# Two small loads at the start of an attention and GEGLU kernel: the last tokens of k and v moved to the hardware queue, and a norm column made by a matmul instead of by element transfers

## The chip, the cores and the metric

One core of a Trainium2 chip. The metric is the device time of one execution in microseconds (us), given as the median of several runs. The kernel before takes 358.03 us (three runs, 357.89 to 358.11). The profile is taken of one of these runs; its span, from the first to the last instruction, is about 1.7 us shorter than the time of the same run.

## The reference

```python
def _attn_ref(q, k, v, g_norm):            # q, k, v: (8, 8, 576, 64) fp32; g_norm: (64,)
    kv = np.einsum('bhsd,bhse->bhde', k, v)
    out = np.einsum('bhsd,bhde->bhse', q, kv)
    rms = np.sqrt(np.mean(out * out, axis=-1, keepdims=True) + 1e-06)
    return (out / rms * g_norm).astype(np.float32)

# x = attention's result, as 4608 tokens x 512 channels
def _moe_ref(x, w_gate, w_val, w_out, w_res):   # (512,1536), (512,1536), (1536,512), (512,512)
    g = x @ w_gate
    gelu = 0.5 * g * (1.0 + erf(g / sqrt(2)))
    ffn_out = gelu * (x @ w_val) @ w_out
    res_gate = 1.0 / (1.0 + np.exp(-(x @ w_res)))
    return (x + res_gate * ffn_out).astype(np.float32)
```

Each batch has 576 tokens: four tiles of 128, and 64 last tokens that the kernel treats apart.

## The kernel before

The long part of the kernel is a chain of fp16 matmuls that keeps the tensor engine (PE) full. Only the start matters here: until batch 0 has passed through the attention, PE has nothing to chew. The loads of batch 0 go out on three queues. SP issues q, k and v in halves of four heads, in fp32, on a hardware queue. GpSimd issues the last tokens of k and v on the software queue, which casts to fp16 on the way. ACT issues g_norm twice: as a row, and as a column of 128 partitions with one 4-byte element in each.

```python
    def load_last_kv(b):
        for tile_, t in zip(last_kv[b % 2], (k, v)):
            nc.gpsimd.dma_start(out=tile_[0:R], in_=t[b, :, M0:S, :].rearrange("h s d -> s h d"))
    ...
    def load_first(which, t, half):
        hs = slice(half * HH, (half + 1) * HH)
        nc.sync.dma_start(out=raw[0, which][:, hs, :], in_=rows4(t, 0, hs.start, hs.stop))

    for half in range(2):
        for which, t in (("q", q), ("k", k), ("v", v)):
            load_first(which, t, half)
    load_last_kv(0)
    grow = consts.tile([1, D], FP32, name="grow")
    nc.scalar.dma_start(out=grow, in_=g_norm.unsqueeze(0))
    gcol = consts.tile([P, 1], FP32, name="gcol")
    for e in range(2):
        nc.scalar.dma_start(out=gcol[e * D : (e + 1) * D, :], in_=g_norm.unsqueeze(1))
```

The order of the first work follows. `keep_warm` issues matmuls of zeros ("fillers") that are meant to keep PE's clock up. `hold` makes GpSimd wait for the first k/v product before it issues the weights, so that these don't compete with q, k and v.

```python
    keep_warm(7)
    ...
    f_cast("q", 0, HH, nc.scalar.copy)
    f_qT(0)
    f_cast("k", 0, HH, nc.vector.tensor_copy)
    f_qT_out(0, nc.scalar.copy)
    f_qT_out(1, nc.scalar.copy)
    nc.vector.tensor_copy(out=g16, in_=gps)
    f_cast("v", 0, HH, nc.vector.tensor_copy)
    keep_warm(7)
    f_kv(0)                      # per head pair: 4 matmuls of v and k, 1 of their last tokens
    f_kv_out(0)
    ...
    hold = consts.tile([1, 1], FP16, name="hold")
    nc.gpsimd.tensor_copy(out=hold, in_=s0["kv2"][0:1, 0, 0:1])
    load_wg(0)
    load_wv(0)
    f_cast("k", HH, H, nc.gpsimd.tensor_copy)
    for i in range(1, len(WCS)):
        load_wg(i)
        load_wv(i)
```

Of the kernel before, what the change touches and what calls it, by code (L numbers as in the profile page):

```python
# [8 lines left out]
FP32 = mybir.dt.float32  # L9
# [9 lines left out]
def kernel(  # L19
# [15 lines left out]
    nc = tc.nc  # L35
    P = nc.NUM_PARTITIONS
    B, H, S, D = q.shape
# [5 lines left out]
    M0 = NJ * P  # L43
    R = S - M0
    RP = R // NJ
    HH = H // 2
    WCS = (256, 256, 512, 512)

    consts = ctx.enter_context(tc.tile_pool(name="consts", bufs=1))
# [10 lines left out]
    pattn = ctx.enter_context(tc.tile_pool(name="pattn", bufs=4, space=bass.MemoryType.PSUM))  # L60
# [11 lines left out]
    def rows4(t, b, lo, hi):  # L72
        return t[b, lo:hi, 0:M0, :].rearrange("h (p j) d -> p h (j d)", j=NJ)
# [10 lines left out]
    last_kv = [[consts.tile([P, H, D], FP16, name=f"{n}l{i}") for n in "kv"] for i in range(2)]  # L84
# [4 lines that stand above are left out]
# [33 lines left out]
    def load_wg(i):  # L122
        load_columns(wg_c, moe_w_gate, i)

    def load_wv(i):
        load_columns(wv_c, moe_w_val, i)
# [295 lines left out]
    for which in "kv":  # L422
        t = hidp.tile([P, NF, NJ * P], FP16, tag="hid", name=which + "f")
        t = t.rearrange("p a b -> p (a b)").bitcast(FP32)
        raw[0, which] = t[:, 0 : H * NJ * D].rearrange("p (h x) -> p h x", h=H)

    def load_first(which, t, half):
        hs = slice(half * HH, (half + 1) * HH)
        nc.sync.dma_start(out=raw[0, which][:, hs, :], in_=rows4(t, 0, hs.start, hs.stop))

    for half in range(2):
        for which, t in (("q", q), ("k", k), ("v", v)):
            load_first(which, t, half)
    load_last_kv(0)
    grow = consts.tile([1, D], FP32, name="grow")
    nc.scalar.dma_start(out=grow, in_=g_norm.unsqueeze(0))
    gcol = consts.tile([P, 1], FP32, name="gcol")
    for e in range(2):
        nc.scalar.dma_start(out=gcol[e * D : (e + 1) * D, :], in_=g_norm.unsqueeze(1))
    ident32 = consts.tile([P, P], FP32, name="ident32")  # L440
    make_identity(nc, ident32)

# [9 lines left out]
    nc.vector.memset(eps_col, RMS_EPS)  # L452
    ones16 = consts.tile([1, P], FP16, name="ones16")
    nc.vector.memset(ones16, 1.0)
    ident = consts.tile([P, P], FP16, name="ident")
    nc.vector.tensor_copy(out=ident, in_=ident32)

    qtr = [consts.tile([P, NP, P], FP16, name=f"qtr{i}") for i in range(2)]
    grow16 = consts.tile([1, H, D], FP16, name="grow16")
    nc.vector.tensor_copy(out=grow16, in_=grow[:, None, :].to_broadcast([1, H, D]))  # L460
    for t in last_kv[1] + qtr:
# [5 lines left out]
    def keep_warm(n):  # L467
        for _ in range(n):
            nc.tensor.matmul(idle, lhsT=zeros[:, 0:P], rhs=zeros, start=True, stop=True)
# [10 lines left out]
    def f_cast(which, lo, hi, copy):  # L480
        hs = slice(lo, hi)
        dst, src = b16_t[0, which], raw[0, which]
        if which == "v":
            copy(out=dst[:, hs, :], in_=src[:, hs, :])  # L484
        else:
            copy(
                out=dst.rearrange("p j h d -> p h j d")[:, hs, :, :],
                in_=src.rearrange("p h (j d) -> p h j d", j=NJ)[:, hs, :, :],
            )

    def f_qT(half):
        q16 = b16_t[0, "q"].rearrange("p j h d -> p j (h d)")
        for e2 in range(2):
            pr = 2 * half + e2
            first["qT", pr] = ps = pattn.tile([P, NJ, P], FP16, tag="at", name="qtp")
            for j in range(NJ):
                nc.tensor.transpose(ps[:, j, :], q16[:, j, pr * P : (pr + 1) * P], ident)

    def f_qT_out(pr, copy):
        copy(out=s0["qT"][:, :, pr, :], in_=first["qT", pr])  # L500
# [81 lines left out]

    keep_warm(7)

    g16 = consts.tile([P, C], FP16, name="g16")
    gps = pattn.tile([P, C], FP32, tag="at", name="gbp")
    nc.tensor.matmul(gps, lhsT=ones16, rhs=grow16.rearrange("p h d -> p (h d)"), start=True, stop=True)
# [3 lines that stand above are left out]
    f_qT_out(0, nc.scalar.copy)  # L591
    f_qT_out(1, nc.scalar.copy)
    nc.vector.tensor_copy(out=g16, in_=gps)
    f_cast("v", 0, HH, nc.vector.tensor_copy)
    keep_warm(7)
    f_kv(0)
# [8 lines left out]
    load_wg(0)  # L605
    load_wv(0)
    f_cast("k", HH, H, nc.gpsimd.tensor_copy)
    for i in range(1, len(WCS)):
        load_wg(i)
        load_wv(i)  # L610
# [208 lines left out]
```

## Time and profile before

| quantity, kernel before | value |
|---|---|
| median time | 358.03 us |
| span of the profiled run | 356.6 us |
| first half of v landed | 10.60 us |
| first k/v product starts | 11.37 us |
| first block of the value weights landed | 19.12 us |
| PE starts the third column block of the gate product | 25.89 us |

Two views matter most. That of busy time by stretches gives for every microsecond the busy time of PE, weight load, DVE, ACT and GpSimd, then the granted PE clock (1.00 is full speed), the DMA share (the mean over the 16 engines; it can pass 1.00) and the GB/s moved. The chain of waits gives start, length and what of the work that set the end. The prediction below shows the lines of both for the kernel before.

### The profile page before, as it was taken

What the parts mean: (1) busy time and instruction counts of PE and PEld (TensorE: products, weight loads), DVE (VectorE), ACT (ScalarE), POOL (GpSimd) and SP (SyncE); (2) the same over time, 40 slices, a digit from 0 to 9 for tenths busy, and PEclk for the clock granted to TensorE, in tenths of its full rate; (3) what the DMA queues carried; (4) which work ended last, traced back from release to release, by engine and by line L of the source; (5) the groups of instructions that cost most, each with busy time, mean ns of one, the idle gap of its engine ahead of it and who ended that gap; (6) DMA issues with size and microseconds to landing.
All of it is one profiled execution on the core that took longest, in us unless ns stands there. A gap on an engine that the chain in (4) does not pass through costs nothing.

```text
span 356.6 us, 5012 instructions
## 1 busy us (share of the span) xinstructions
PE 344.9 (97%) x1903; PEld 169.4 (48%) x1903; DVE 214.4 (60%) x425; ACT 125.7 (35%) x215; POOL 47.3 (13%) x72
## 2 busy tenths in 40 slices
PE   7869999999999999999999999999999999999995
PEld 2454465454455445544454445444544444444443
DVE  4555438877847865685569755855587544343433
ACT  3463374343236312531264224422542233223320
POOL 2563150050041003200050014000000000000000
PEclk9999999999999999999999999999999999999998
DMA  7999999289489055914896279518000500020013
GB/s 189 242 181 202 193 204 158 89 148 140 119 159 174 2 132 124 186 9 107 146 131 71 68 182 153 47 46 178 29 2 29 132 31 0 29 88 3 1 31 88
DMA packets 77835, 37.82 MB, mean 106 GB/s; under 512 B 42354, under 2 KB 73330, under 8 KB 77810
## 3 DMA queue, kind: packets, MB, share of 16 engines
q0 software_dynamic: 40848, 17.83, 39.9%
q1 hardware_dynamic: 36640, 19.53, 21.8%
q8 instruction: 15, 0.25, 0.3%
q10 hardware_dynamic: 322, 0.13, 0.2%
q14 instruction: 10, 0.08, 0.1%
HBM read 38.80 MB, written 9.44 MB: 135 GB/s over the span
## 4 chain that ended last, share of the span: by engine, by line
PE 91%; DMA 4%; DVE 1%; ACT 1%; issue 0%; SPq 0%; POOL 0%; DVEq 0%
PE gps L315 26%; PE vps L315 26%; PE fps L348 25%; PE rps L335 9%; DMA vf<-in_v_dram 2%; PE kvp L165 2%; PE op L194 2%; DMA wv<-in_moe_w_val_dram 2%; PE fps L377 1%; PE orp L212 1%; PE kvp L172 0%; ACT xT L581 0%; DVE hid L304 0%; ACT L664 0%; ACT xT L265 0%
## 5 line engine op out<-in xcount | busy, mean ns | idle before, releaser
L315 PE MATMUL gps<-xT,wg 128*128 128x512 f16 (+2 forms) x448 | 112.3, 371 | 2.3 <-ACT xT L581 1.2
L315 PE MATMUL vps<-xT,wv 128*128 128x512 f16 (+2 forms) x448 | 112.3, 371 | 0.8 <-DMA wv<-in_moe_w_val_dram 0.8
L304 DVE TENSOR_TENSOR hid<-ge,vps 128x512 f16<-128x512 f16 x108 | 73.5, 685 | 65.7 <-PE vps L315 57.7
L303 ACT ACTIVATE ge<-gps 128x512 f16<-128x512 f32 x108 | 64.5, 598 | 114.2 <-PE gps L315 105.2
L348 PE MATMUL fps<-wo,hid 128*128 128x512 f16 x420 | 96.8, 379 | 0.0
L315 PEld LDWEIGHTS <-wv 128*128 128x128 f16 x448 | 43.4, 98 | 51.2 <-DMA wv<-in_moe_w_val_dram 1.1
L348 PEld LDWEIGHTS <-hid 128*128 128x128 f16 x420 | 40.8, 98 | 47.9
L315 PEld LDWEIGHTS <-wg 128*128 128x128 f16 x448 | 42.1, 98 | 44.0 <-issue 2.7
L354 DVE SCALAR_TENSOR_TENSOR pf<-th,fps 128x512 f32<-128x512 f32 x35 | 23.8, 687 | 47.9 <-PE fps L348 47.9
L344 ACT ACTIVATE th<-rps 128x512 f32<-128x512 f32 x36 | 21.5, 598 | 79.5 <-PE rps L335 79.5
L335 PE MATMUL rps<-wr,xT 128*128 128x512 f16 x144 | 36.5, 379 | 0.0
L188 DVE TENSOR_REDUCE ss<-sq 128x8 f32<-128x512 f32 x32 | 21.5, 684 | 6.2 <-ACT sq L187 4.3
L359 DVE SCALAR_TENSOR_TENSOR osb<-pf,t 128x512 f32<-128x512 f32 x35 | 24.2, 691 | 1.1
L335 PEld LDWEIGHTS <-xT 128*128 128x128 f16 x144 | 14.1, 98 | 17.0
L187 ACT ACTIVATE sq<-op 128x512 f32<-128x512 f32 x28 | 16.8, 598 | 9.8 <-PE op L194 8.8
L705 POOL COPY hold<-qT 1x1 f16<-1x1 f16 x5 | 0.9, 178 | 140.4 <-DMA qT<-q 140.4
L252 DVE TENSOR_TENSOR t<-op,ny 128x512 f16<-128x512 f32 x28 | 17.8, 681 | 0.1
L271 DVE TENSOR_TENSOR t<-t,g 128x512 f16<-128x512 f16 x36 | 13.3, 417 | 0.0
L165 PE MATMUL kvp<-v,k 128*128 128x128 f16 x128 | 10.5, 219 | 1.5 <-DVE v L484 1.3
L165 PEld LDWEIGHTS <-k 128*128 128x128 f16 x128 | 9.0, 98 | 5.6 <-issue 2.3
L194 PEld LDWEIGHTS <-qT 128*128 128x128 f16 x112 | 8.4, 98 | 5.7
L194 PE MATMUL op<-kv,qT 128*128 128x128 f16 x112 | 10.8, 219 | 0.0
(89 smaller groups left out, 169.1 us busy)
## 6 DMA issues: line engine op xcount, KB each, us to landing
out_dram<-osb SPq DMA_DIRECT2D x32, 256.0 KB, 2.4
qraw<-in_q_dram POOLq DMA_DIRECT2D x7, 512.0 KB, 6.0
kraw<-in_k_dram POOLq DMA_DIRECT2D x7, 512.0 KB, 8.4
v<-in_v_dram POOLq DMA_DIRECT2D x7, 512.0 KB, 10.3
wo<-in_moe_w_out_dram POOLq DMA_DIRECT2D x3, 512.0 KB, 14.0
qf<-in_q_dram SPq DMA_DIRECT2D x2, 512.0 KB, 7.1
kf<-in_k_dram SPq DMA_DIRECT2D x2, 512.0 KB, 8.5
vf<-in_v_dram SPq DMA_DIRECT2D x2, 512.0 KB, 9.4
```

Source lines behind the costliest of these rows:

```text
L165: nc.tensor.matmul(ps, lhsT=k16[:, j, cs], rhs=v16[:, 2 * pr : 2 * pr + 2, j * D : (j + 1) * D], start=(j == 0), stop=False,)
L188: nc.vector.tensor_reduce(out=st[b]["ss"][:, j, :], in_=sq, op=ALU.add, axis=mybir.AxisListType.X)
L194: nc.tensor.matmul(ps[:, pr * P : (pr + 1) * P], lhsT=s["qT"][:, j, pr, :], rhs=s["kv2"][:, pr, :], start=True, stop=True)
L252: nc.vector.tensor_tensor(out=t_t[blk][:, jj, :].rearrange("p (h d) -> p h d", h=H), in0=s["o"][j].rearrange("p (h d) -> p h d", h=H), in1 ...
L303: nc.scalar.activation(out=ge, in_=gps, func=AF.Gelu)
L304: nc.vector.tensor_tensor(out=hids[blk][:, f, :], in0=ge, in1=vps, op=ALU.mult)
L315: nc.tensor.matmul(ps[:, j0 * P : j1 * P], lhsT=w[:, cc, :], rhs=xT_t[blk][:, j0:j1, cc, :], start=(cc == 0 and j0 == 0), stop=(cc == NP - ...
L335: nc.tensor.matmul(rps, lhsT=xT_t[blk][:, j, cc, :], rhs=wr16[:, cc, :], start=(cc == 0), stop=(cc == NP - 1),)
L344: nc.scalar.activation(out=th, in_=rps, func=AF.Tanh, scale=0.5)
L348: nc.tensor.matmul(fps, lhsT=hids[blk][:, f, j * P : (j + 1) * P], rhs=wo16[:, f, :], start=(f == 0), stop=(f == NF - 1))
L354: nc.vector.scalar_tensor_tensor(out=pf, in0=th, scalar=1.0, in1=fps, op0=ALU.add, op1=ALU.mult)
L359: nc.vector.scalar_tensor_tensor(out=osb, in0=pf, scalar=0.5, in1=t_t[blk][:, j, :], op0=ALU.mult, op1=ALU.add)
```

## The change

The intent is to take small transfers away from the first 12 us: the last tokens of k and v of batch 0 are loaded in fp32 by SP, in front of the matching halves of v, and cast by GpSimd; the column of g_norm is made on PE, as the row (twice, 1x128) times a 1x1 one.

```diff
-    for half in range(2):
-        for which, t in (("q", q), ("k", k), ("v", v)):
-            load_first(which, t, half)
-    load_last_kv(0)
+    last_raw = [consts.tile([R, H, D], FP32, name=f"{n}lf") for n in "kv"]
+
+    def load_first_last(i, half):
+        hs = slice(half * HH, (half + 1) * HH)
+        nc.sync.dma_start(
+            out=last_raw[i][:, hs, :], in_=(k, v)[i][0, hs, M0:S, :].rearrange("h s d -> s h d")
+        )
+
     grow = consts.tile([1, D], FP32, name="grow")
     nc.scalar.dma_start(out=grow, in_=g_norm.unsqueeze(0))
-    gcol = consts.tile([P, 1], FP32, name="gcol")
-    for e in range(2):
-        nc.scalar.dma_start(out=gcol[e * D : (e + 1) * D, :], in_=g_norm.unsqueeze(1))
+    for half in range(2):
+        load_first("q", q, half)
+        load_first("k", k, half)
+        load_first_last(0, half)
+        load_first_last(1, half)
+        load_first("v", v, half)
 ... (cut: one32 = 1.0; grow32 = the row twice in fp32)
+    def f_cast_last(half):
+        hs = slice(half * HH, (half + 1) * HH)
+        for i in range(2):
+            nc.gpsimd.tensor_copy(out=last_kv[0][i][0:R, hs, :], in_=last_raw[i][:, hs, :])
 ... (cut)
     keep_warm(7)
 
+    gcol = consts.tile([P, 1], FP32, name="gcol")
+    gcp = pattn.tile([P, 1], FP32, tag="at", name="gcp")
+    nc.tensor.matmul(gcp, lhsT=grow32.rearrange("p h d -> p (h d)"), rhs=one32, start=True, stop=True)
+    nc.vector.tensor_copy(out=gcol, in_=gcp)
 ... (cut)
+    f_cast_last(0)
     f_cast("v", 0, HH, nc.vector.tensor_copy)
 ... (cut)
     f_cast("k", HH, H, nc.gpsimd.tensor_copy)
+    f_cast_last(1)
```

More of the change, by code (lines that the diff above doesn't have):

```diff
@@ L454 @@
     nc.vector.memset(ones16, 1.0)
+    one32 = consts.tile([1, 1], FP32, name="one32")
+    nc.vector.memset(one32, 1.0)
     ident = consts.tile([P, P], FP16, name="ident")
@@ L458 @@
     qtr = [consts.tile([P, NP, P], FP16, name=f"qtr{i}") for i in range(2)]
+    grow32 = consts.tile([1, 2, D], FP32, name="grow32")
+    nc.vector.tensor_copy(out=grow32, in_=grow[:, None, :].to_broadcast([1, 2, D]))
     grow16 = consts.tile([1, H, D], FP16, name="grow16")
```

## The prediction

> **What bounds the kernel now.** I read the page first, then the chain of waits, the busy time of the engines in one-microsecond stretches, the timeline of the first 26 us, and the list of DMA issues. By the stretches the kernel has two parts:
>
> ```profile
> 0.00:1.00 1.00, 0.00 (x0) 0.00 (x0) 0.14 (x1) 0.27 (x1) 0.20 (x4) 1.00 0.00 0
> ...
> 40.00:340.00 300.00, 299.82 (x1629) 145.51 (x1628) 187.72 (x364) 106.02 (x182) 29.43 (x43) 1.00 0.57 95
> ```
>
> The columns are the stretch and its length, busy time of PE, weight load, DVE, ACT and POOL, then the granted clock, the DMA share and GB/s. From 40 to 340 us PE is busy 299.82 of 300 us: nothing in the diff touches that part, so it can only be moved as a block. What the change is worth is how much sooner the block starts, that is, when PE begins the third column block of the gate product, at 25.89 us. The chain of waits says what sets that moment (start, length, what):
>
> ```profile
> 1.79 8.81 DMA vf<-in_v_dram
> ...
> 10.62 0.70 DVE v L484
> ...
> 11.37 0.38 PE kvp L165 x4
> ...
> 12.13 0.43 DVE kv L508
> ...
> 12.79 0.72 POOL wg L120
> 13.51 5.61 DMA wv<-in_moe_w_val_dram
> ...
> 25.89 1.02 PE gps L315 x4
> ```
>
> Two transfers carry the first 19 us: the first half of v, landing at 10.60, and the first block of the value weights, landing at 19.12. The second isn't independent: GpSimd issues it only after the first kv product is out (12.55 us), so it moves with v. Between 19.12 and 25.89 a chain of PE, ACT and DVE work follows.
>
> What delays v? The same view, early:
>
> ```profile
> 3.00:4.00 1.00, 1.00 (x4) 0.17 (x2) 0.55 (x3) 0.00 (x0) 0.29 (x1) 1.00 1.02 322
> 4.00:5.00 1.00, 0.89 (x2) 0.10 (x1) 0.90 (x4) 0.00 (x0) 0.00 (x0) 1.00 1.06 358
> 5.00:6.00 1.00, 0.00 (x0) 0.00 (x0) 0.19 (x1) 0.93 (x1) 0.00 (x0) 1.00 0.71 144
> 6.00:7.00 1.00, 0.83 (x9) 0.83 (x10) 0.00 (x0) 0.30 (x2) 0.00 (x0) 1.00 1.04 200
> 8.00:9.00 1.00, 1.00 (x4) 0.30 (x3) 0.79 (x2) 0.00 (x0) 0.00 (x0) 1.00 1.12 222
> ...
> 11.00:12.00 1.00, 0.63 (x11) 0.63 (x11) 0.32 (x1) 0.00 (x0) 0.00 (x0) 1.00 1.09 383
> ```
>
> The rate is 322 to 358 GB/s, falls to 144 to 225 from 5 to 9 us with the DMA engines as busy as before, and is back at 383 after 11 us. The transfers whose landing brackets the dip are the small ones:
>
> ```profile
> kl<-in_k_dram POOLq DMA_DIRECT2D x1, 64.0 KB, 6.7
> vl<-in_v_dram POOLq DMA_DIRECT2D x1, 64.0 KB, 9.4
> gcol<-in_g_norm_dram ACTq DMA_DIRECT2D x2, 0.2 KB, 6.9
> ```
>
> Issued at 1.24 and 2.02 us, the last tokens of k and v land at 7.9 and 11.4. The last is beyond v's own 10.60 and only 0.17 us ahead of the matmul that uses it (11.59).
>
> **What the Trainium skill says.** "DMA: Bandwidth & Descriptors", section "Queues, rings and completion order": every DMA engine takes the queues with work in turn, packet by packet, so small packets on a second queue hold up big ones on the first. The dip agrees in direction; the trace doesn't show the turns. Same page, "Specifications": under 512 B a transfer doesn't run at line rate. "TensorE: Matmul & The Clock Gate", "Part 1: The HAM clock gate": the array runs at half rate until it has been busy for a free-running window of about 3.4 us. The trace agrees: weight loads of the 128x512 fillers start 0.427 us apart at 7.43 to 9.56 us, while nine fillers from 13.77 take 2.11 us, 0.234 each. "SBUF — State Buffer", "SBUF: two separate sides": GpSimd and a DVE cast in its two-port mode lock each other out. In the trace the GpSimd cast of k (14.25 to 15.31) and a DVE cast of v (15.13, 0.73 against 0.69 alone) overlap by 0.18 us and DVE loses 0.04, so I see little of it here.
>
> **The change part by part.**
>
> *Removed from the software queue:* 2 x 512 packets of 256 B. The software queue's 40848 packets took 39.9% of 16 x 356.6 us = 2277 us. Counting the rows of the tiles, 23552 are 1 KB reads and 4096 are 2 KB reads. At a share of 1.33 and 170 GB/s landed (15 to 21 us), a 1 KB read costs an estimated 64 ns, and I take 90 for 2 KB. That leaves about 400 us for 12288 small ones, an estimate of 33 ns each. So 1024 x 33 / 16 = 2.1 us of every DMA engine, almost all before v's first half lands.
>
> *Removed from the Activation queue:* 128 element packets. That queue's 322 packets took 0.2% = 11.4 us, 35 ns each: 128 x 35 / 16 = 0.3 us. The two issues' 1.18 us on ACT are hidden, as ACT waits for q until 5.07.
>
> *Added on SP's queue, ahead of each half of v:* 2 x 256 packets of 256 B. The only hardware 256 B packets here are the transposes: 1244 us for that queue, less some 530 for loads and stores, over 28.9 thousand, estimated 25 ns. 512 x 25 / 16 = 0.8 us before v's first half, 0.8 more before its second. Issuing costs SP 0.5 us each, but only kl and vl's two (1.0 us) stand before v, which then is issued near 2.8 us; the queue before it holds data until after 6 us, so this is hidden.
>
> *First half of v.* Data starts near 1.95 us. Three 0.524 MB halves at 350 GB/s are 4.5 us, plus 0.8, gives 7.25; q's landing (5.04 against some 3.9 by summed bytes) shows about 1.1 us from last bytes to landing, so v lands at 8.4 to 9.2 instead of 10.6. The DVE cast (0.69) then ends by 9.1 to 9.9.
>
> *What takes the wait over:* PE's own fillers. The timeline:
>
> ```profile
> 7.00 3.06 PE L469 MATMUL idle<-zeros 128*128 128x512 f16 x7
> 11.37 0.38 PE L165 MATMUL kvp<-v,k 128*128 128x128 f16 x4 [1.32 <-DVE v L484]
> ```
>
> They stand before the kv product in PE's order, begin after q's transposes (which hang on q's landing, first in its queue in both versions) and end at 10.06. So of 1.4 to 2.2 us that v gains, PE can use 11.37 - 10.08 = 1.3 us. POOL's casts of kl and vl (256 columns; 1.06 us for 1024, so some 0.3 each) end near 8 us, hidden.
>
> *Second half of v.* It stays last in the hardware queue: 1.95 + 6 x 1.5 + 1.6 = 12.55 us of data, landing 13.7 to 14.0 instead of 15.06. DVE is free for that cast at 15.07 now, at about 13.7 after. So this allows 1.1 to 1.4 us as well, nearly a tie.
>
> *Second k/v product:* GpSimd gets two casts, 0.6 us, after its cast of k. They end near 14.6, when PE wants them; any 0.3 us lost sits before transposes that wait for DVE anyway.
>
> *Weights:* issued 1.3 us sooner (12.7 to 11.4), so the value block lands near 17.8, 1.3 sooner, a few tenths more since the hardware loads are then almost over. The later blocks are issued after the 0.6 us of casts, net 0.7 us sooner; by then they have slack (the second gate block lands at 20.4, used at 25.89).
>
> *Small parts:* the one-column matmul, its copy, a memset and a 128-element cast cost DVE about 0.4 us between 2.5 and 6 us, when it next waits for k (7.5). Hidden.
>
> *Sum:* 1.3 us sooner at the kv product, 1.1 to 1.4 at v's second half, 1.3 to 1.6 at the weights. I take 1.4 us by these, less 0.2 because the kv product now may start while the array is still cold: its ten 128-column matmuls would cost about 0.5 us more at half rate, and I give that a little under one chance in two. 358.03 - 1.2 = **356.8 us**.
>
> **The rivals.**
> 1. *The casts and GpSimd take the wait.* The second pair of casts delays both the product and the later weights. For: GpSimd is busy without gaps from 12.6 to 22 us, and shares its port with DVE. Against: 0.6 us, at a place with slack. It would leave 0.6 to 0.8 us: 357.3.
> 2. *256 B packets are as slow in the hardware queue.* They now stand in series in front of v rather than beside it. At 60 ns each v's halves land at 9.6 and 16, the second later than today. For: the packets are no bigger. Against: transposes' 25 ns. Time 357.6 to 358.8.
> 3. *The weights are late.* The first software transfer of the kernel is then the weights' own; if the queue starts slowly the first time (kl took 6.7 us for 64 KB), the value block stays at 19 us and nothing is gained: 358.0.
> 4. *The chain is loosened further.* Without hardware traffic beside them the weights land near 17 us, q's second half comes 1.5 us sooner and ACT's squares no longer wait behind its cast (13.17, products ready at 12.95): 2 us or more, 355.8.
>
> **Range and chances.** The part before 26 us is all there is to win: even 3 us would be 0.8%, and a loss of 2% (7.2 us) has no mechanism. Runs of the kernel agree within 0.22 us. Rivals 1 to 3 reach to 358, rival 4 to 355.8; I put the range at **356.0 to 357.8**. Faster by over 2%: 0.005; within 2%: 0.99; slower: 0.005.
>
> **What would show it right or wrong.** Right: no dip of GB/s from 5 to 9 us; v landing near 9; the kv product starting straight after the seven fillers, near 10.1, with no wait for DVE; GpSimd's first weight issue near 11.4; the value block landing near 17.8; the first 128x512 gate matmul of the third block near 24.6; then 299.8 of 300 us busy as before. Wrong: the kv product waits for v's cast or for GpSimd (rival 2 or 1), matmuls 0.107 us apart in it (the clock), the second cast of v long after DVE is free (the queue's order), or an unchanged landing of the value block (rival 3).

## More of the kernel before

One view it doesn't show is that of the DMA queues (packets, MB, share of the 16 engines' time):

```profile
q10 hardware_dynamic: 322, 0.13, 0.2%
```

This is ACT's queue: 322 packets that take almost nothing.

## The result, and the profile after

The changed kernel took 356.13 us (four runs, 355.88 to 356.94) against 358.07 (four runs, 357.89 to 358.58) of the kernel before. The ratio is 0.9948, with a 95% interval of 0.9928 to 0.9967. Ratios in this document are the mean time of one kernel's fast runs over that of the other's of the same rounds, so not quite the ratio of the medians quoted. The gain of 0.5% is clear of zero. The profiled span went from 356.6 to 354.6 us.

Busy time by stretches of the kernel after:

```profile
5.00:6.00 1.00, 0.39 (x7) 0.39 (x8) 0.00 (x0) 0.55 (x1) 0.00 (x0) 1.00 1.20 311
6.00:7.00 1.00, 1.00 (x10) 0.53 (x7) 0.90 (x2) 0.96 (x2) 0.35 (x1) 1.00 1.10 247
7.00:8.00 1.00, 0.74 (x4) 0.13 (x2) 0.40 (x1) 0.12 (x1) 0.44 (x2) 1.00 1.09 353
8.00:9.00 1.00, 0.00 (x0) 0.00 (x0) 0.64 (x1) 0.00 (x0) 0.00 (x0) 1.00 1.08 382
...
40.00:340.00 300.00, 299.21 (x1625) 145.30 (x1624) 186.24 (x362) 105.28 (x181) 29.41 (x43) 1.00 0.55 95
```

The stretch from 5 to 9 us, where the kernel before moved 144 to 225 GB/s, now moves 247 to 382. Over these four microseconds that is 1.29 MB, and was 0.79: 0.50 MB more, nearly one of the two loads of v (0.52 MB). The long part is as full as before but for 0.6 us.

The chain of waits of the kernel after:

```profile
3.25 5.09 DMA vf<-in_v_dram
...
8.36 0.71 DVE v L495
...
9.11 0.40 PE kvp L165 x4
...
11.39 0.76 POOL wv L120
12.15 1.04 POOL k L497
13.20 0.34 POOL kl L505
13.53 0.87 POOL vl L505
...
33.14 13.88 DMA wo<-in_moe_w_out_dram
```

v lands at 8.34 instead of 10.60, the product starts at 9.11 instead of 11.37. Then the chain goes another way than before: through GpSimd's casts and its weight issues to the output weights (w_out). The timeline shows what that costs (the bracket is the idle time ahead and what ended it):

```profile
13.11 0.43 POOL L505 CAST kl<-klf 64x256 f16<-64x256 f32 x1
13.45 0.95 POOL L505 CAST vl<-vlf 64x256 f16<-64x256 f32 x1
13.46 0.69 DVE L495 CAST v<-vf 128x1024 f16<-128x1024 f32 x1 [0.77 <-DMA vf<-in_v_dram]
...
23.35 1.02 PE L315 MATMUL gps<-xT,wg 128*128 128x512 f16 x4 [0.85 <-ACT ge L303]
...
47.07 1.04 PE L348 MATMUL fps<-wo,hid 128*128 128x512 f16 x4 [0.60 <-DMA wo<-in_moe_w_out_dram]
```

The third column block starts at 23.35 instead of 25.89, 2.54 us sooner. At 47.07 PE waits 0.60 us for the first block of w_out. 2.54 less 0.60 is 1.94, which is the 2.0 us of the span. In this trace w_out is issued at 33.14, and was at 34.03: it moved by only 0.9 us, as the second gate block did, which is issued behind the casts (14.35, was 15.24), while PE moved by 2.5.

So the number fell inside the range. Whether its reasons hold is another matter: the prediction put nearly all of the gain on moving the last tokens, and 0.3 us on the element transfers. Both parts were in one diff, and the landing of both lies around the dip.

### The profile page after: what moved, and what is told of

Same layout as the page of the kernel before. It is cut to its first block, busy times and chain, and to the rows that moved or that the text cites. A ratio compares the mean times of both kernels' runs of the same rounds, so it can differ in the third digit from the quotient of the medians.

```text
span 354.6 us, 5021 instructions
## 1 busy us (share of the span) xinstructions
PE 343.0 (97%) x1905; PEld 168.9 (48%) x1905; DVE 214.1 (60%) x428; ACT 125.7 (35%) x215; POOL 47.7 (13%) x74
## 4 chain that ended last, share of the span: by engine, by line
PE 84%; DMA 9%; POOL 2%; DVE 1%; SPq 1%; ACT 0%; issue 0%; DVEq 0%
PE fps L348 25%; PE gps L315 23%; PE vps L315 23%; PE rps L335 8%; DMA wv<-in_moe_w_val_dram 4%; DMA wo<-in_moe_w_out_dram 4%; PE op L194 2%; PE kvp L165 2%; DMA vf<-in_v_dram 1%; POOL wg L120 1%; PE fps L377 1%; POOL wv L120 1%; PE orp L212 1%; PE kvp L172 0%; SPq L435 0%; DVE hid L304 0%
## 5 line engine op out<-in xcount | busy, mean ns | idle before, releaser
L252 DVE TENSOR_TENSOR t<-op,ny 128x512 f16<-128x512 f32 x28 | 17.8, 680 | 0.1
```

The source lines that it names most:

```text
L252: nc.vector.tensor_tensor(out=t_t[blk][:, jj, :].rearrange("p (h d) -> p h d", h=H), in0=s["o"][j].rearrange("p (h d) -> p h d", h=H), in1 ...
```

## The experiments

The theory (T) is that the software queue's 256-byte packets held up v. The rival (R) is that the element transfers did, though they count for 0.2% of DMA time. A later pair concerns why: by the size of the packets, by their number, or because all of them read the same place. Eleven experiments ran, in three calls, each on a chip of its own with runs of the kernel before between them. All gave correct results but one that is wrong. Times are medians of several runs, but landings and starts are of one trace each. In the five that have the last tokens and no element transfers beside v, it landed at 8.34 to 8.63; in the two of the kernel before at 10.60 and 9.89. So a difference of 0.3 us between single traces shows little.

| kernel | median us (range, runs) | ratio to before, 95% | v landed | third block |
|---|---|---|---|---|
| **first chip:** before | 358.08 (357.21–359.05, 11) | 1 | | |
| after again | 356.21 (355.77–357.05, 6) | 0.9950 (0.9932–0.9968) | 8.44 | 23.65 |
| last tokens alone | 357.32 (356.87–357.82, 6) | 0.9979 (0.9962–0.9996) | 9.52 | 24.94 |
| column alone | 356.08 (355.89–356.45, 6) | 0.9944 (0.9928–0.9960) | 8.47 | 23.54 |
| second casts on ACT | 356.00 (355.75–356.89, 6) | 0.9946 (0.9927–0.9965) | 8.41 | 23.57 |
| **second chip:** before | 357.69 (357.31–358.22, 7) | 1 | | |
| half the elements | 357.83 (357.04–358.18, 4) | 0.9999 (0.9982–1.0015) | 9.87 | 24.53 |
| rows instead of elements | 358.38 (357.91–358.48, 4) | 1.0014 (0.9999–1.0029) | 10.36 | 25.48 |
| 128 spread elements | 356.00 (355.75–357.48, 4) | 0.9961 (0.9934–0.9988) | 8.65 | 23.58 |
| 256 spread elements | 356.34 (355.82–356.87, 4) | 0.9960 (0.9944–0.9976) | 9.00 | 23.38 |
| **third chip:** before | 358.25 (357.77–358.46, 7) | 1 | | |
| no last tokens (wrong result) | 356.91 (356.66–358.56, 4) | 0.9976 (0.9948–1.0004) | 7.71 | 24.42 |
| elements behind the loads | 356.38 (356.00–356.61, 4) | 0.9948 (0.9933–0.9963) | 8.63 | 24.02 |
| before again | 358.29 (357.50–358.66, 4) | 0.9999 (0.9983–1.0015) | 9.89 | 26.09 |

"v landed" is the end of the load of v's first half, "third block" the start of the first 128x512 gate matmul, both in us of the profiled run.

### The two parts of the change apart

**After again.** No edit.

> The changed kernel again, unaltered. Theory: 2.5 us sooner at the start of the steady part, 0.6 given back waiting for the first block of w_out, so about 1.9 us faster (ratio near 0.995). Clock rival: the profile of the changed kernel had its second seven fillers at full rate (1.68 us), the profile of the kernel before had them at half rate (3.06 us), and both kernels issue the same fillers up to 4.2 us, so this may be chance. If the clock made much of the gain, then a profile with slow fillers (about 3.06 us) shows the kv product near 9.6 rather than 9.1 us, and times spread by about 0.5 us or more; if it made little, the time stays within 0.2 us of 356.1.

It repeats the gain. Its trace differs in one way from the first: the fillers ran cold. Timeline:

```profile
6.48 2.92 PE L480 MATMUL idle<-zeros 128*128 128x512 f16 x7
...
9.24 0.39 PE L165 MATMUL kvp<-v,k 128*128 128x128 f16 x4
...
13.57 0.42 POOL L505 CAST vl<-vlf 64x256 f16<-64x256 f32 x1
13.60 0.94 DVE L495 CAST v<-vf 128x1024 f16<-128x1024 f32 x1 [0.79 <-DMA vf<-in_v_dram]
```

Seven fillers in 2.92 us here, in 1.68 in the first trace of the same kernel. Here they end at 9.40, as the prediction had feared, and the product starts a hair later (9.24 for 9.11; the ends of matmuls are modelled, so the two overlap). There is no wait for w_out. And the two casts that collide share the loss the other way: GpSimd's took 0.42 and DVE's 0.94, in the first trace 0.95 and 0.69. (GpSimd's cast need not be the only reason: DVE's cast took 0.91 in the run with the second casts on ACT, when GpSimd was issuing weights.)

**Last tokens alone.**

```diff
 (the changed kernel, with)
+    gcol = consts.tile([P, 1], FP32, name="gcol")
+    for e in range(2):
+        nc.scalar.dma_start(out=gcol[e * D : (e + 1) * D, :], in_=g_norm.unsqueeze(1))
 (and without the matmul, grow32 and one32)
```

> Only the last tokens of k and v moved to the hardware queue with GpSimd casts; g_norm's column by two element transfers as before. Theory (small software packets made the dip): nearly the whole gain, 1.5 to 1.9 us faster, v's first half lands below 9 us, no dip from 5 to 9 us. Rival (the element transfers of g_norm made the dip): the dip stays, v lands at 9.5 or later, gain below 1 us. Third possibility: with three more transfers [...]SP's sixth transfer must wait for its first (q, near 5 us) and the next one for an element transfer of g_norm; then v's second half comes later than 13.4 us and part of the gain is lost.

Only 0.76 us of some 2 (358.08 to 357.32). The dip is still there, with the software queue empty. By stretches:

```profile
5.00:6.00 1.00, 0.31 (x6) 0.32 (x7) 0.00 (x0) 0.63 (x1) 0.00 (x0) 1.00 0.46 130
6.00:7.00 1.00, 1.00 (x10) 0.54 (x8) 0.85 (x2) 0.88 (x2) 0.00 (x0) 1.00 0.70 189
...
12.00:13.00 1.00, 1.00 (x13) 1.00 (x11) 0.00 (x1) 0.74 (x3) 1.00 (x2) 0.50 1.14 205
```

130 and 189 GB/s in the two microseconds in which the trace has the element packets, from 4.7 to 6.9 us. The DMA share falls to 0.46: in more than half of the engines' time no packet is recorded, so they aren't full of small packets. The third line shows a second loss, the granted clock at 0.50 after PE had idled 2.48 us for v's cast. And the third possibility came true in part: SP waited for k and q, so that v's second half was issued at 8.01 (in the changed kernel 6.51) and landed at 15.1. What of the missing gain is due to each wasn't tested apart; PE, with fillers at half rate before it, came to the second k/v product only at 15.94.

**Column alone.**

```diff
 (the kernel before, with)
-    gcol = consts.tile([P, 1], FP32, name="gcol")
-    for e in range(2):
-        nc.scalar.dma_start(out=gcol[e * D : (e + 1) * D, :], in_=g_norm.unsqueeze(1))
 (and with the matmul, grow32 and one32 of the changed kernel; the last tokens stay on the software queue)
```

> Only g_norm's column by a matmul; the last tokens by the software queue with cast as before. Theory: at most 0.3 us of every DMA engine is saved, v's first half lands at 10.2 to 10.6, the last tokens' v still lands near 11, so 0 to 0.3 us faster (358.07 to 357.7). Rival (the element transfers made the dip): 1 us or more faster, v lands below 9.5.

This has the whole gain: 356.08, with the full change at 356.21 in the same rounds. By stretches:

```profile
5.00:6.00 1.00, 0.29 (x5) 0.18 (x4) 0.33 (x3) 0.77 (x1) 0.00 (x0) 1.00 1.64 278
6.00:7.00 1.00, 1.00 (x12) 0.64 (x10) 0.59 (x1) 0.74 (x2) 0.00 (x0) 1.00 1.18 314
...
8.00:9.00 1.00, 0.00 (x0) 0.00 (x0) 0.51 (x1) 0.00 (x0) 0.00 (x0) 1.00 1.28 304
```

The software queue's small packets run just as before and the dip is gone. A share of 1.64 (1.02 from the software queue, 0.62 from SP's) shows packets of two queues open in one engine at a time: the small ones lie beside the big ones, mostly not in front of them. The last tokens of v landed at 9.5 here, and at 11.4 before. So the late landing that the prediction read as a cause was itself held up. The theory T falls for the greater part, and R holds.

The parts do not add: alone they give 0.76 and 2.00 us, together 1.87. Moving the last tokens pays only while the stall is there.

**No last tokens (wrong result).**

```diff
 (column alone, with)
-    load_last_kv(0)
-        nc.vector.memset(t[R:P], 0.0)
+        nc.vector.memset(t, 0.0)
```

> A wrong result on purpose (the last 64 tokens of batch 0 are left out of its kv product): g_norm's column by a matmul, and the last tokens of k and v of batch 0 not loaded at all. It measures what the 1024 small packets of the software queue cost v's first half. My prediction took 2.1 us of every DMA engine for them, so v would land at 8.5 - 2.1 = 6.4 us. If they mostly fill gaps beside the hardware queue, it lands at 7.4 to 8.2 us, and the time is 355.2 to 356.0.

This measures what is left of T. Without any small packet v landed at 7.71; with the software ones at 8.47 (column alone), with the hardware ones at 8.34 (the change). The last tokens thus cost v some 0.76 us on the software queue and 0.63 on the hardware queue. These are single traces on different chips; elements behind the loads, on the same chip as this run, gives 8.63 and so 0.92 for the software queue. That the sooner landing brought no time was a miss. Timeline:

```profile
7.73 0.69 DVE L484 CAST v<-vf 128x1024 f16<-128x1024 f32 x1 [0.35 <-DMA vf<-in_v_dram]
...
16.46 0.39 PE L315 MATMUL vps<-xT,wv 128*128 128x256 f16 x2 [0.88 <-DMA wv<-in_moe_w_val_dram]
...
19.10 0.63 PE L315 MATMUL gps<-xT,wg 128*128 128x256 f16 x2
```

The value weights, issued at 10.75, took 5.67 us and so landed hardly sooner than in the changed kernel (16.42, there 16.58). PE then ran at half rate: the pair of gate matmuls takes 0.63 instead of 0.38, and the granted clock between 18 and 22 us is 0.50 to 0.70. That isn't the whole of it: two of the four runs have a mean clock of 1.000 and took 356.86 and 356.66, still not less than column alone. The rest stays open.

### Why do element transfers of 512 bytes cost two microseconds?

**128 spread elements.** As many packets, as small, on the same queue at the same time, but each from another row of w_out:

```diff
 (column alone, with)
+    dummy = consts.tile([P, 1], FP32, name="dummy")
+    for e in range(2):
+        nc.scalar.dma_start(out=dummy[e * D : (e + 1) * D, :], in_=moe_w_out[e * D : (e + 1) * D, 0:256:256])
```

> g_norm's column by a matmul as in the change, the last tokens by the software queue as before, and two transfers of 64 single elements each, from 128 different rows of w_out, into a tile that nobody reads. If single elements hurt wherever they come from, v lands near 10.6 us and the gain of the matmul (2 us) is gone, 358.0. If only reading one place 128 times hurts, v lands near 8.5 and the time is 356.1.

**256 spread elements.** The same with two elements of each row (`0:512:256`).

> As the run before with two elements per partition, so 256 element packets in the same two transfers. If the cost is a fixed time per element packet, v lands about another 2.1 us later, near 12.7 us, and the kernel takes about 360; if the cost is per transfer, as with 128.

Neither brings the stall back: 356.00 and 356.34. v landed at 8.65 and 9.00, against 8.47 for column alone: 0.18 us for 128 spread elements and 0.53 for 256. The 0.18 can't be told from nothing, as elements behind the loads, with none in front of v, has 8.63. By stretches, with 128:

```profile
5.00:6.00 1.00, 0.50 (x3) 0.19 (x3) 0.33 (x3) 0.76 (x1) 0.00 (x0) 1.00 1.64 267
...
8.00:9.00 1.00, 1.00 (x4) 0.38 (x3) 0.33 (x1) 0.00 (x0) 0.00 (x0) 1.00 1.30 291
...
12.00:13.00 1.00, 1.00 (x10) 0.53 (x8) 0.74 (x2) 0.73 (x3) 1.00 (x3) 1.00 0.49 114
```

**Rows instead of elements.** 128 packets of 256 bytes, all of the one row that g_norm is; the diagonal is picked out on the chip:

```diff
 (the kernel before, with)
-        nc.scalar.dma_start(out=gcol[e * D : (e + 1) * D, :], in_=g_norm.unsqueeze(1))
+        nc.scalar.dma_start(out=grows[e * D : (e + 1) * D, :], in_=g_norm.unsqueeze(0).to_broadcast([D, D]))
 (and, before hold, GpSimd multiplies two 64x64 blocks by the identity; DVE sums the rows after f_t(0, 0, 2))
```

> The kernel before with the same two transfers on the same queue, but each of the 128 packets reads g_norm's whole row of 256 B (the same 256 B for all 128), and GpSimd and DVE pick the diagonal. If the size of the packet is what hurts, v lands near 8.5 to 8.9 us (the packets cost only their own 20 to 30 ns, 0.2 us per engine). If reading one place of HBM 128 times is what hurts, v lands near 10.6 as before.

The stall is as deep as before. By stretches:

```profile
5.00:6.00 1.00, 0.27 (x5) 0.27 (x6) 0.20 (x1) 0.68 (x1) 0.00 (x0) 1.00 0.70 136
...
8.00:9.00 1.00, 0.00 (x0) 0.10 (x1) 1.00 (x2) 0.00 (x0) 0.00 (x0) 1.00 1.08 219
```

Rows of 256 bytes from one place stall the loads (v at 10.36), elements of 4 bytes from 128 places don't. From 5 to 9 us 0.80 MB landed here and 0.79 in the kernel before, with 128 spread elements 1.12. So, beside these loads, it is not the size of the packets and not their number, but where they read. What this pair leaves open is whether any one place would do, or something about where this small tensor lies.

**Half the elements.**

```diff
 (the kernel before, with)
-    for e in range(2):
-        nc.scalar.dma_start(out=gcol[e * D : (e + 1) * D, :], in_=g_norm.unsqueeze(1))
+    nc.scalar.dma_start(out=gcol[0:D, :], in_=g_norm.unsqueeze(1))
 (and a copy of the upper half by ACT after hold)
```

> The kernel before with one of the two element transfers of g_norm's column (64 packets of 4 B instead of 128); the other 64 partitions are filled by a copy on ACT. If each element packet holds its DMA engine up by a fixed time (128 of them made v's first half 2.1 us late, 8 per engine, so about 0.26 us each), v lands halfway, near 9.5 us, and the kernel is about 1 us faster. If it is a cost per transfer or per queue, v lands at 10.6 as before or at 8.5 as without.

Inconclusive. The dip is shorter (107 GB/s from 5 to 6 us; the 64 packets lie between 4.7 and 7.0 us, the 128 of before between 4.7 and 9.3), but v landed at 9.87, hardly sooner than in a run of the kernel before on the third chip (9.89), and the times are those of before. In three of its four runs the mean granted clock was 0.995 and the time 357.82 to 358.18; in the fourth, the profiled one, 0.999 and 357.04. In that trace the third block starts at 24.53, half way between the kernel before and column alone, and 0.91 MB landed from 5 to 9 us, between 0.79 and 1.17. So the trace hints at half the effect, but the times don't show it.

**Elements behind the loads.** The same 128 elements, on SP's queue, where they come after the six loads:

```diff
 (the kernel before, with)
-        nc.scalar.dma_start(out=gcol[e * D : (e + 1) * D, :], in_=g_norm.unsqueeze(1))
+        nc.sync.dma_start(out=gcol[e * D : (e + 1) * D, :], in_=g_norm.unsqueeze(1))
```

> The kernel before with the two element transfers of g_norm's column moved from ACT's queue to the end of SP's, behind the six loads. If 128 reads of one row hold up whatever is in flight beside them, v's first half lands near 8.5 us as without them, and the stall moves to about 12 to 15 us, where the first weight blocks are: the first value block, which lands at 16.8 without them, comes at 18 to 19 us, and most of the gain is lost (357 to 358). If they hurt only beside the hardware loads of the start, the time is 356.1.

I had expected most of the gain to be lost; it is nearly all there, 356.38. Nor does the trace show a stall that moved. From 12 to 13 us, where most of the element packets now run, 87 GB/s were landed at a DMA share of 0.40:

```profile
12.00:13.00 1.00, 1.00 (x10) 0.53 (x8) 0.70 (x2) 0.75 (x2) 1.00 (x3) 1.00 0.40 87
```

But the run with 128 spread elements, where nothing reads one row, has 114 GB/s at 0.49 in the same microsecond (the last line of its fence above): there the loads end and the weights begin. The value weights landed at 17.25, 5.10 us after their issue; with 128 spread elements it was 4.5, over all runs 4.4 to 5.7 us. So that the elements hold the weights up a little is possible, and not shown. The third block starts at 24.02, some 0.4 to 0.7 us later than in the other good versions; in this trace the first k/v product is late too (9.62). The same transfers are dear in front of v and cheap here. One word of the kernel, the name of the queue, gives a ratio (0.9948) that can't be told from that of the whole change.

### The remaining parts

**Second casts on ACT.** The first pair of casts stays on GpSimd, the second goes to ACT behind its square roots:

```diff
 (the changed kernel, with)
-    f_cast_last(1)
     ... 
     f_sqrt(0, 2, 2)
+    f_cast_last(1, nc.scalar.copy)
```

> The changed kernel with the second half's two casts (k and v, last tokens) on ACT instead of GpSimd. Theory (the casts, 1.3 us on GpSimd with one of them held 0.55 us by a DVE cast, delay the software stream of weights, so the first block of w_out lands at 47.0 and PE waits 0.6 us for it): the second gate block is issued near 13.2 instead of 14.35, w_out lands about 1 us sooner, the 0.6 us wait is gone, 0.4 to 0.7 us faster than the changed kernel (355.4 to 355.7). Rival (the stream is bound by its own DMA rate and not by when it is issued): w_out lands within 0.3 us of 47.0 and the time stays at 356.1.

The weight issues come sooner (second gate block at 13.18, in the changed kernel 14.35; w_out at 31.5, there 33.14) and nothing waits for w_out. The time, 356.00, can't be told from 356.21; the 0.4 to 0.7 us expected were a miss. So GpSimd's casts cost at most a few tenths.

**Before again.** No edit.

> The kernel before again, for a second profile: ratio 1.000 within 0.2%; the dip of the rate from 5 to 9 us again, v's first half at 10.3 to 10.7 us. Its second seven fillers may take 1.7 or 3.1 us[...].

Same time and the same dip (144, 202, 227 and 242 GB/s from 5 to 9 us), but here it isn't v that PE waits for at the end:

```profile
11.91 0.22 PE L172 MATMUL kvp<-vl,kl 128*128 128x128 f16 x1 [0.87 <-DMA vl<-in_v_dram]
```

v landed at 9.89 and the last tokens of v at 11.87. In the trace that the prediction used, these landed 0.17 us ahead of their use; here they were the wait. So v's own landing varies between traces of one kernel by 0.7 us, and moving the last tokens alone (0.76 us) may pay because it gets them out of the stall; that wasn't tested apart.

**The clock.** Each timed run has a mean granted clock. Three traces have one of 0.995 and show the drop behind it. For last tokens alone the clock was 0.92, 0.50, 0.50, 0.50 and 0.87 in the five microseconds from 10 to 15, which is half speed for 3.4 us (0.5 x 3.4 / 356 is 0.005); for rows it was nearly the same, after PE had idled 3.26 us for v's cast; for no last tokens it fell from 18 to 22 us. Of the kernel before, 13 of 25 runs have 0.995 or less (and 1 of 4 of before again); of five versions without the stall (both runs of the changed kernel, column alone, casts on ACT, elements behind the loads: 26 runs) none; but of the two with spread elements 2 of 8, and of no last tokens 2 of 4. On the first chip the five such runs of before have a mean of 358.28 us, its other six 357.80. If all had been of the second kind its mean would be 0.22 us lower. So a tenth of the gain may be a clock that no longer falls. This is an estimate and not shown: the two groups overlap (the six reach 358.86), and no trace of the kernel before caught a drop.

## Why the prediction was right or wrong

The range, 356.0 to 357.8, held the result, 356.13; the gain was 1.9 us and not 1.2. The cause on which it rested did not hold. That the range held all the same is in part luck: the diff took away both small loads, so it didn't matter which of them made the dip.

- **"Removed from the Activation queue: 128 x 35 / 16 = 0.3 us".** This is the term that failed. Taking just these transfers away brought v from 10.60 (9.89 in the second trace) to 8.47, and the whole 2.0 us of time. The sum itself is off, as its 35 ns are a mean with the 1 KB packets at the end of the span; at some 8 ns it would be under 0.1 us. Either way the working took the duration of the packets themselves. Nothing in it could see what they do to packets of other queues.
- **"Removed from the software queue: 1024 x 33 / 16 = 2.1 us of every DMA engine".** Measured as the difference between column alone and no last tokens: 0.76 us (0.92 against elements behind the loads). Dividing a queue's packet time by 16 takes it that engines work on one packet at a time; the share of 1.64 shows that they don't.
- **"Added on SP's queue: 0.8 us before v's first half".** Measured 0.63. So the net of the move, once the stall is gone, is 0.1 to 0.3 us for v, not 1.3.
- **"The transfers whose landing brackets the dip are the small ones".** True, and the element transfers are in the same fence, with 6.9 us. Choosing the bigger ones by their bytes was the mistake; the dip lasts about as long as the element packets do (4.7 to 9.3 us in the kernel before, 4.7 to 6.9 in last tokens alone). And "the DMA engines as busy as before" passes over the 0.71 at the start of the dip.
- **"v lands at 8.4 to 9.2".** It was 8.34 and 8.44 in two traces. This sum doesn't use the two terms above: it takes the full rate of 350 GB/s, the packets added (0.8) and the way to the landing (1.1). It needs only that the dip goes, whatever made it.
- **"PE's own fillers take the wait over".** Half right, and the cap of 1.3 us that it sets did not hold: the product moved by 2.26 and 2.13 us (9.11 and 9.24, was 11.37). The fillers "hang on q's landing", and q landed sooner (4.51, was 5.04), so that they begin at 6.07 and 6.48 instead of 7.00. In one trace they run cold and end as the product starts; in the other they run at full rate, end by 7.75 and PE waits 1.37 us for v's cast. Which of the two happens differs between runs of one kernel. Elements behind the loads had cold fillers too: they end at 9.82, and its product starts at 9.62, 0.28 us after v's cast was over (8.65 + 0.69), at half rate (0.63 us for four matmuls, otherwise 0.38 to 0.40).
- **"Second half of v landing 13.7 to 14.0".** 13.41 measured; right for the purpose.
- **"GpSimd gets two casts, 0.6 us".** From the start of the first to the end of the second they took 1.29 us, as the second sat behind DVE's cast of v. The prediction had read the lock off a case that showed 0.04 us; in the second trace of the kernel before the same DVE cast took 1.03 us, 0.34 more than alone. It named the place as one with slack, which holds but for w_out.
- **"The value block lands near 17.8".** 16.58. The first weight issue was expected near 11.4 and came at 10.49; the value block was issued at 11.38, 2.13 us sooner than before (13.51) and not 1.3, as it hangs on the product; on the way it took 5.20 us instead of 5.61. Together that is 2.54 us, just what the third block moved by (24.6 predicted, 23.35 measured). So most of what the prediction left out is the earlier product. Rival 4, weights that travel faster without loads beside them, would account for 0.4 us at most.
- **Rivals 1 to 3.** PE waited 0.6 us for w_out, issued behind the casts, in one trace and not at all in another (1). The hardware queue's small packets are no worse than the software queue's (2). The value weights weren't late (3).

One small effect was in none of the lists. In the trace of before SP waits 1.2 us for q before it issues its sixth load; in the changed kernel, where it issues ten loads, v's second half still goes out at 6.51. What decides SP's waits was not tested apart.

What stays open is why these reads of one place stall the loads beside them. That they do at the start of this kernel, and not by size or number, is shown; behind the loads they cost nothing that the runs show, and half of them is inconclusive. What in the memory or the engines does it, no run here shows.

Among column alone, casts on ACT and the full change no difference is shown (356.00 to 356.21, with ranges over each other). A simple one, the column by a matmul with the last tokens left where they were, is enough; the elements moved behind the loads are simpler still and gave the same ratio on another chip (0.9948).

## What to carry to other kernels

This kernel shows it for one small tensor only; it is worth a check elsewhere. Before tuning big transfers, look for small ones that read the same few bytes many times (a vector spread over the partitions, a row broadcast) beside a stream that something waits for: load one row once and spread it on the chip, or issue it behind that stream. Judge such a transfer by what the others do while it runs, and not by its bytes or its share of DMA time. The sign is a low rate while it runs. The DMA share need not be low with it: it was 0.46 in last tokens alone, but 0.71 to 1.12 in the kernel before, where other small packets filled it up. And when a diff has two parts that end in the same stretch, let each run alone before a cause is written down, even when the predicted number was met.

## What the Trainium skill lacked or had wrong

- "DMA: Bandwidth & Descriptors", section "Latency and other measured facts", tells of slow copies at large power-of-two row pitches and calls aliasing in the memory an inference. It has nothing on many reads of one small row. Here 128 reads of one 256-byte row, in 4-byte elements or as whole rows, cut what landed from 5 to 9 us to 0.79 to 0.98 MB (kernel before twice, rows, last tokens alone); the runs without them that have the last tokens landed 1.08 to 1.29. Against column alone this made v 1.4 to 2.1 us late; 128 reads of as many rows, 0.18 us.
- The same page, section "Specifications": under 512 bytes a transfer isn't at line rate. The runs don't contradict it, but size didn't decide here: 128 packets of 4 bytes from spread rows were nearly free, 128 of 256 bytes from one row were the dear ones.
- The same page, section "Queues, rings and completion order": engines take queues in turn, packet by packet. The runs don't contradict it, but a DMA share of 1.64 shows packets of two queues open at once in one engine, and the small packets cost v 0.76 us where turns taken strictly one after the other made my estimate 2.1.
- "SBUF — State Buffer", section "SBUF: two separate sides": the lock goes to whichever instruction starts first, and the other waits. The runs agree that one of the two pays: GpSimd's cast took 0.95 us (0.39 alone) beside a DVE cast of 0.69, and in another run 0.42 beside one of 0.94. Who comes first couldn't be read here: the records start 0.01 and 0.03 us apart, GpSimd's first both times.
- "TensorE: Matmul & The Clock Gate", section "Part 1: The HAM clock gate": a free-running window. The runs agree: the same seven fillers took 1.68 us in one run and 2.92 in another of the same kernel, and after 2.48 us of idling the granted clock was 0.50 for some 3.4 us.
